# Two order lists for the start of a fused attention and MLP kernel: with two exponentials per unit, three MLP pieces in the list, and one doubling on GpSimd

## The chip, the cores and the metric

The kernel runs on one core of a Trainium2 chip. The time is device microseconds (us) of one execution. The core has engines that each work through their own instructions in order and meet through semaphores: TensorE (PE, with its weight loads shown as PEld), VectorE (DVE), ScalarE (ACT), GpSimd (POOL), and SyncE (SP), which here only issues transfers. POOL and ACT can issue transfers too.

## The reference

Eight batches, 12 heads, 448 positions, head size 64, model size 768, hidden size 3072. Cut to what matters:

```python
def rmsnorm(x, g):
    rms = np.sqrt(np.mean(x * x, axis=-1, keepdims=True) + 1e-06)
    return x / rms * g
q_n, k_n = rmsnorm(q, g_q), rmsnorm(k, g_k)
attn = softmax(q_n @ k_n.T / sqrt(64))        # per batch and head
x = concat_heads(attn @ v)                    # (8, 448, 768)
xn = (x - mean(x)) / np.sqrt(var(x) + 1e-06) * g_ln
out = x + np.maximum(xn @ w_ch1, 0.0) @ w_ch2 # 768 -> 3072 -> 768
```

## The kernel before

Heads are taken in pairs: 6 pairs per batch, 48 in all, numbered p = 0 to 47. Loading and preparation go by unit u: units 0 and 1 are one pair each, every other unit is two pairs (unit 4 is pairs 6 and 7, unit 5 is pairs 8 and 9). The 448 positions of a pair are cut into 7 groups: three of 128 per head and one with the last 64 of both heads.

Preparation of a unit has pieces with one-letter names (`pieces`, L188):

- `b` takes tiles, `a` squares k and `c` squares q (ACT), `d` and `e` sum these squares over the 64 elements of a row (DVE);
- `g` (`root`, L219) makes one over the root of both sums on ACT: a logarithm, then an exponential. Units 0 and 1 do this with 7 columns per kind, the others with 14. In the kernel before, one exponential makes both kinds, 128x28;
- `i` multiplies k with both gains (POOL from unit 2 on), `j` rounds it to 16 bits (POOL for units 1 to 5, then ACT), `k` makes the 16-bit rest (DVE);
- `l` scales q into `qn` (DVE), `m` doubles `qn` (POOL for units 1, 2 and 4, DVE for the others);
- `z` converts v (POOL). `L` loads a unit (SP); a load waits until the buffer of the unit two before it has been read.

For a pair, `K` and `Q` transpose keys and queries on PE into PSUM and copy them out (DVE; ACT for queries of pairs 0 and 1). `Sp.i` is a score matmul of group i and the exponential on ACT that reads its PSUM; the PSUM tiles of scores are two in turn, so score i+2 of the sequence waits for exponential i. The root of the keys is the exponential's scale, one number per row, so it is read long after unit preparation. `Vp.i` multiplies with the values; after `Vp.6`, DVE divides and writes the result into x (`evac_o`, L395: four instructions). `T` are statistics of x for the layer norm, `A` their sum, `N0` to `N2` the normalised rows of three tiles (DVE), `X0` to `X2` their transposes (PE) with copies (ACT, ACT, DVE), `R` the layer norm's root (ACT). `U0` to `U2` are the first three of 24 up pieces of the first MLP, one third of the columns at a time, in three PSUM tiles of a pool of three; the pieces after these use the same pool.

The order of the start, up to and including pair 6, is a list written out by hand, `ORDER` (L36). Every engine gets its instructions in the list's order. It holds batch 0's attention, the layer norm, pair 6, and the preparation of unit 5. After it, `run_rest` (L708) takes the MLP pieces of batch 0: 21 up pieces (6 matmuls 128x384 and a ReLU on ACT each) and 24 down pieces (6 matmuls each), and puts the attention steps of batch 1 between them:

```python
upto(int(min(goal, start + (goal - start) * done / (total - 960 * tail))))
```

`done` is the cost so far and `tail` is 13 pieces, so the 44 steps of batch 1 are spread evenly over the first 45 - 13 = 32 pieces. Step 1 is `b6 a6 i6` and the load of the first half of the down weights (`load_w2`, L529, issued by POOL behind `i6`); step 3 is `c6 S7.0`. The other half of the down weights comes with `a7 i7`. From pair 12 on DMA makes the transposes.

At the list's end, `M` makes two small numbers for a final test of ranges. With it come reductions `least` (L364): the least key root of a unit goes into `rr_all`, 25 columns, five of them at `M` for units 0 to 4, the others at the end of each unit's first pair. `flag` (L736) tests them in the last MLP.

Of the kernel before, what the change touches and what calls it, by code (L numbers as in the profile page):

```python
# [25 lines left out]
UNIT_PAIR = [PAIR_UNIT.index((u, 0)) for u in range(len(UNITS))]  # L26
EXP_BIAS = -4.0
WARM = 22
DVE_KG, POOL_HI, POOL_DUP, ACT_Q = (0, 1), (1, 2, 3, 4, 5), (1, 2, 4), (0, 1)

# [1 line left out]


ORDER = """  # L36
b0 a0 c0 L4 i0 j0 e0 k0 gq0 l0 b1 m0 a1 c1 K0 Q0 d0 G gk0 S0.0 S0.1 d1 e1 L5 i1 g1 j1 l1 k1 m1
z0 b2 a2 S0.2 d2 c2 S0.3 S0.4 K1 V0.0 e2 i2 S0.5 Q1 g2 l2 S0.6 S1.0 j2 V0.1 S1.1 S1.2 m2 b3
V0.2 a3 V0.3 k2 c3 S1.3 K2 V0.4 S1.4 z2 V0.5 Q2 S1.5 V0.6 V1.0 i3 W0 d3 e3 S1.6 V1.1 V1.2 S2.0
j3 T0 V1.3 S2.1 S2.2 Q3 V1.4 S2.3 K3 S2.4 V1.5 V1.6 S2.5 g3 z3 S2.6 V2.0 S3.0 S3.1 V2.1 k3  # L40
S3.2 b4 S3.3 V2.2 l3 a4 V2.3 m3 S3.4 V2.4 K4 S3.5 Q4 V2.5 V2.6 S3.6 Q5 S4.0 V3.0 S4.1 V3.1 i4
V3.2 d4 T1 K5 V3.3 W1 c4 V3.4 V3.5 S4.2 S4.3 V3.6 S4.4 S4.5 W2 e4 V4.0 V4.1 j4 S4.6 S5.0 k4
S5.1 g4 V4.2 l4 S5.2 V4.3 V4.4 V4.5 S5.3 K6 V4.6 z4 V5.0 S5.4 m4 b5 V5.1 G2 S5.5 L6 V5.2 S5.6
V5.3 V5.4 V5.5 Q6 a5 i5 V5.6 T3 T4 S6.0 S6.1 S6.2 S6.3 T5 S6.4 A V6.0 V6.1 N0 V6.2 N1 V6.3
S6.5 S6.6 d5 V6.4 X0 X1 U0 N2 R Q7 X2 c5 e5 j5 g5 k5 l5 z5 U1 U2 V6.5 M m5 V6.6 L7 K7
""".split()
DMA_UNIT = 8
PE_SET = (DMA_UNIT + 1) % 2
# [27 lines left out]
class _Fast:  # L76


    def __init__(self, ctx, tc, sh, q, k, v, gs, g_ln, w1, w2, out):
        self.gs, self.g_ln = gs, g_ln  # L80
        self.tc, self.nc, self.sh = tc, tc.nc, sh
        self.q, self.k, self.v, self.w1, self.w2, self.out = q, k, v, w1, w2, out
        nc = tc.nc
        pool = lambda name, bufs, **kw: ctx.enter_context(tc.tile_pool(name=name, bufs=bufs, **kw))
        self.p_in = pool("p_in", 2)
        self.p_n = pool("p_n", 2)
        self.p_e = pool("p_e", 2)
# [100 lines left out]
    def pieces(self, u):  # L188
# [29 lines left out]

        def root(n=slice(0, 2)):  # L219
            nc.scalar.activation(c["rt"][:, n], c["ssq"][:, n], AFT.Ln, bias=D * 1e-6)  # L220
            nc.scalar.activation(c["rb"][:, n], c["rt"][:, n], AFT.Exp, scale=-0.5)  # L221
# [85 lines left out]
    def trans_k(self, p):  # L307
        nc, sh = self.nc, self.sh
        u, w = PAIR_UNIT[p]
        qn, khl = self.units[u][0:2]  # L310
        kT, ps = self.kU[PE_SET][:, 960 * (p % 2):960 * (p % 2) + 960], self.tr
        nc.tensor.matmul(ps[:, 0:256].rearrange("p (e o) -> p e o", e=2)[:, :, 0:D],
                         khl[:, self.group(p, 6)], sh.id16, is_transpose=True, start=True, stop=False)
# [3 lines left out]
        nc.vector.tensor_copy(out=kT, in_=ps[:, 0:960])

    def trans_q(self, p):
        nc, sh = self.nc, self.sh  # L320
        u, w = PAIR_UNIT[p]
        qn, khl = self.units[u][0:2]
        tr = self.ps_m.tile([128, 1024], FP16, tag="mlp", name="psQ") if p < NPAIR else self.tr
        ps = tr[:, 128:128 + 2 * S].rearrange("p (e s) -> p e s", e=2)
        qT = self.qU[PE_SET][:, p % 2].rearrange("p e s -> p (e s)")
        nc.tensor.matmul(ps[:, :, 384:S], qn[:, self.group(p, 6)], sh.id16, is_transpose=True,
                         start=True, stop=False)
        for i in range(6):
            nc.tensor.matmul(ps[:, i // 3, ts(i % 3, 128)], qn[:, self.group(p, i)], sh.id16,  # L329
                             is_transpose=True, start=False, stop=(i == 5))  # L330
        if p in ACT_Q:
            nc.scalar.copy(out=qT, in_=ps.rearrange("p e s -> p (e s)"))
        else:
            nc.vector.tensor_copy(out=qT, in_=ps.rearrange("p e s -> p (e s)"))  # L334
        kT = self.kU[PE_SET][:, 960 * (p % 2):960 * (p % 2) + 960]
        self.prs[p] = dict(q=qT, main=kT[:, 192:960], left=kT[:, 0:192])

    def scores(self, p, i):
# [17 lines left out]
        g = self.group(p, i)  # L356
        nc.scalar.activation(out=c["E"][:, i], in_=ps[:, 0:S], func=AFT.Exp,  # L357
                             scale=self.units[PAIR_UNIT[p][0]][3][:, g:g + 1], bias=EXP_BIAS)
# [62 lines left out]
    def first_attention(self):  # L421
# [7 lines left out]
        for x in ORDER:  # L429
# [517 lines left out]
```

## Time and profile before

| what | value |
|---|---|
| median of 4 runs | 610.15 us (609.79 to 610.46) |
| the profiled execution | 609.62 us, span 607.9 us |
| PE busy | 579.5 us of the span |
| DVE, ACT, POOL busy | 287.1, 359.0, 189.6 us |
| first matmul | 9.81 us after the span's start |
| end of the list (last matmul of `K7`) | 59.60 us |

The page gives busy times and their share of the span by engine. Stretches ("windows") give the busy time of each engine between two times; the timeline gives instructions in order of time, and in brackets how long the engine was idle before one and what ended that. "L351" is a line of the kernel. In the timeline, instructions of the same form that follow each other are merged; a single one's duration can overlap the next by about 0.1 us, so distances between starts are used for sums.

### The profile page before, as it was taken

The numbers are of one execution on the slowest core, as the hardware profiler recorded it, in microseconds if no ns is written. First come the engines' busy times: TensorE is split into PE (matmuls) and PEld (weight loads), VectorE is DVE, ScalarE is ACT, GpSimd is POOL, SyncE is SP. The second block draws the span as 40 slices with busy tenths as digits, with TensorE's granted clock in tenths as the row PEclk, the third lists the DMA queues.
The fourth block names the chain that finished last, engine by engine and source line by source line (L and its number), as shares of the span: only waits on it lengthen the run. The fifth ranks groups of instructions, "written<-read, shape, count | busy, mean of one in ns | idle before, by whom it ended". The sixth has DMA issues, their size and how long they took to land.

```text
span 607.9 us, 11525 instructions
## 1 busy us (share of the span) xinstructions
PE 579.5 (95%) x4500; PEld 346.3 (57%) x4500; DVE 287.1 (47%) x643; ACT 359.0 (59%) x673; POOL 189.6 (31%) x245
## 2 busy tenths in 40 slices
PE   2777999999999999999999999999999999999995
PEld 1555566655566666655566666655566666654564
DVE  5798577734256255724266246633346322540011
ACT  5896887368843598448754498538754377114200
POOL 2844432232542355332552345514422000000000
PEclk9899999999999999999999999999999999999999
DMA  8999999679965486747865575948613330040011
GB/s 221 272 181 214 198 221 185 89 242 88 131 147 120 103 139 144 178 130 99 117 130 126 114 118 149 191 117 127 135 56 76 92 62 1 27 104 0 1 53 57
DMA packets 130861, 75.29 MB, mean 124 GB/s; under 512 B 96656, under 2 KB 121040, under 8 KB 130800
## 3 DMA queue, kind: packets, MB, share of 16 engines
q1 hardware_dynamic: 114048, 45.12, 38.9%
q0 software_dynamic: 16080, 28.94, 22.2%
q8 instruction: 37, 0.61, 0.4%
q10 hardware_dynamic: 672, 0.43, 0.2%
q14 instruction: 24, 0.20, 0.1%
HBM read 52.36 MB, written 11.01 MB: 104 GB/s over the span
## 4 chain that ended last, share of the span: by engine, by line
PE 89%; DVE 2%; ACT 0%; issue 0%; DVEq 0%
PE psC L647 36%; PE psH L631 35%; PE psS L351 8%; PE oA L389 5%; PE oB L391 2%; PE psS L354 1%; PE psS L355 1%; PE tr L329 0%; PE tr L315 0%; PE psU L677 0%; DVE stat L555 0%; DVE xn L576 0%; DVE x L406 0%; DVE qU L334 0%; ACT E L357 0%
## 5 line engine op out<-in xcount | busy, mean ns | idle before, releaser
L631 PE MATMUL psH<-xnT,w 128*128 128x512 f16 (+1 forms) x1134 | 241.9, 353 | 0.0
L357 ACT ACTIVATE E<-psS,rr_all 128x448 f16<-128x448 f32 x336 | 207.2, 634 | 49.6 <-PE psS L351 44.2
L647 PE MATMUL psC<-w,hT 128*128 128x384 f16 (+1 forms) x1368 | 234.7, 323 | 0.0
L633 ACT ACTIVATE hT<-psH 128x512 f16<-128x512 f32 (+1 forms) x189 | 103.9, 550 | 124.7 <-PE psH L631 123.1
L647 PEld LDWEIGHTS <-hT 128*128 128x128 f16 x1368 | 127.7, 98 | 74.4
L631 PEld LDWEIGHTS <-w 128*128 128x128 f16 x1134 | 102.7, 98 | 80.5
L351 PE MATMUL psS<-qU,kU 128*128 128x448 f16 x288 | 101.0, 358 | 8.0 <-ACT E L357 5.3
L389 PEld LDWEIGHTS <-E 128*128 128x128 f16 x1008 | 71.2, 99 | 48.8 <-issue 4.3
L228 POOL TENSOR_TENSOR qkv<-qkv,gprod 128x896 f32<-128x896 f32 x21 | 43.7, 2079 | 97.2 <-issue 50.6
L389 PE MATMUL oA<-v,E 128*128 128x65 f16 x864 | 67.0, 194 | 0.1
L651 DVE SCALAR_TENSOR_TENSOR x<-psC,rs_all,x 128x384 f32<-128x384 f32 x48 | 29.0, 616 | 71.0 <-PE psC L647 70.5
L404 DVE RECIPROCAL rec_all<-oA 128x6 f32<-128x6 f32 x48 | 9.3, 194 | 94.0 <-PE oA L389 93.8
L391 PE MATMUL oB<-v,E 128*128 128x65 f16 x288 | 52.0, 194 | 0.1
L127 POOL DMA_DIRECT2D qkv<-in_k_dram x14 | 11.2, 797 | 128.9 <-ACT E L357 77.0
L217 DVE TENSOR_REDUCE ssq<-khl 128x14 f32<-128x896 f32 (+1 forms) x24 | 25.6, 1065 | 45.6 <-ACT khl L214 45.5
L351 PEld LDWEIGHTS <-kU 128*128 128x128 f16 x288 | 28.2, 99 | 25.9 <-issue 6.1
L217 DVE TENSOR_REDUCE ssq<-qn 128x14 f32<-128x896 f32 (+1 forms) x25 | 26.1, 1046 | 21.9 <-ACT qn L214 21.8
L67 DVE SCALAR_TENSOR_TENSOR qn<-qkv,rr_all 128x256 f16<-128x256 f32 (+1 forms) x72 | 26.3, 425 | 15.3 <-ACT rr_all L221 15.3
L391 PEld LDWEIGHTS <-E 128*128 128x128 f16 x336 | 32.6, 97 | 0.3 <-DVE xl L411 0.2
L239 DVE TENSOR_TENSOR khl<-qkv,khl 128x896 f16<-128x896 f32 x21 | 22.7, 1083 | 10.6 <-ACT khl L236 6.9
L406 DVE TENSOR_TENSOR x<-oA,rec_all 128x384 f32<-128x384 f32 x48 | 26.8, 558 | 1.5
L555 DVE BATCH_NORM_STATS2 stat<-x 128x6 f32<-128x256 f32 (+1 forms) x75 | 26.2, 404 | 0.6
(104 smaller groups left out, 448.0 us busy)
## 6 DMA issues: line engine op xcount, KB each, us to landing
out_dram<-x SPq DMA_DIRECT2D x20, 384.0 KB, 2.5
qkv<-in_k_dram POOLq DMA_DIRECT2D x14, 384.0 KB, 3.8
qkv<-in_q_dram POOLq DMA_DIRECT2D x14, 384.0 KB, 5.1
qkv<-in_v_dram POOLq DMA_DIRECT2D x14, 384.0 KB, 7.1
w<-in_moe_w_ch_dram POOLq DMA_DIRECT2D x3, 1536.0 KB, 13.1
w<-in_moe_w_ch_dram POOLq DMA_DIRECT2D x2, 2304.0 KB, 25.5
qkv<-in_k_dram SPq DMA_DIRECT2D x7, 384.0 KB, 6.4
qkv<-in_q_dram SPq DMA_DIRECT2D x7, 384.0 KB, 5.9
```

What stands on the lines that cost most here:

```text
L67: nc.vector.scalar_tensor_tensor(out=out, in0=x, scalar=8.0, in1=r.unsqueeze(2).broadcast_to([x.shape[0], g, D]), op0=ALU.mult, op1=ALU.mult)
L217: nc.vector.tensor_reduce(out=c["ssq"][:, n], in_=c["sq", n], axis=AX.X, op=ALU.add)
L228: (nc.vector if u in DVE_KG else nc.gpsimd).tensor_tensor(out=c["t"][1], in0=c["t"][1], in1=sh.gprod.unsqueeze(1).broadcast_to([128, g, D] ...
L351: nc.tensor.matmul(ps[:, 0:S], c["main"][:, ts(i, 128)], q[:, ts(h, S)], start=True, stop=True)
L357: nc.scalar.activation(out=c["E"][:, i], in_=ps[:, 0:S], func=AFT.Exp, scale=self.units[PAIR_UNIT[p][0]][3][:, g:g + 1], bias=EXP_BIAS)
L389: nc.tensor.matmul(oA[:, t, cs], E[:, i, ts(t, 128)], rhs, start=(i == 0 and t == 0), stop=(i == 6 and t == 2))
L391: nc.tensor.matmul(oB[:, cs], E[:, i, 320:448], rhs, start=(i == 0), stop=(i == 6))
L406: nc.vector.tensor_tensor(out=x[:, :, 128 * hp:128 * hp + 128].rearrange("p t (e d) -> p t e d", e=2), in0=oA[:, :, :, 0:D], in1=rec[:, 0: ...
L631: nc.tensor.matmul(ps[:, 0:N], sh.w1[:, dc, ts(f, 128)], xnT[:, dc, 0:N], start=(dc == 0), stop=(dc == NDC - 1))
L633: nc.scalar.activation(out=hT[:, f, 0:N], in_=ps[:, 0:N], func=AFT.Relu)
L647: nc.tensor.matmul(ps[:, 0:g[1]], hT[:, f, ts(t, 128)], sh.w2[:, f, cols], start=(f == 0), stop=(f == NFF - 1))
L651: nc.vector.scalar_tensor_tensor(out=x[:, cols], in0=ps[:, 0:g[1]], scalar=self.rs[:, b, t:t + 1], in1=x[:, cols], op0=ALU.mult, op1=ALU.add)
```

## The change

- The list `ORDER` is another permutation of the same entries, with three new entries `C`. Each `C` emits the next MLP piece of batch 0 (up pieces 3, 4 and 5). One stands between `U2` and `V6.5`, one between `V6.6` and `R` (before `K7`), and one is the last entry.
- `run_rest` gets what is left: 18 up and 24 down pieces. The 44 steps of batch 1 are spread over 42 - 13 = 29 pieces.
- `m5` goes to POOL.
- `root` makes two exponentials, one for queries into a tile of two buffers, one for keys into `rr_all`, which now has a column for every row group of every pair (336). `least` is gone with its 25 reductions; `flag` tests 336 columns directly.

```diff
-DVE_KG, POOL_HI, POOL_DUP, ACT_Q = (0, 1), (1, 2, 3, 4, 5), (1, 2, 4), (0, 1)
+DVE_KG, POOL_HI, POOL_DUP, ACT_Q = (0, 1), (1, 2, 3, 4, 5), (1, 2, 4, 5), (0, 1)
 ORDER = """
-b0 a0 c0 L4 i0 j0 e0 k0 gq0 l0 b1 m0 a1 c1 K0 Q0 d0 G gk0 S0.0 S0.1 d1 e1 L5 i1 g1 j1 l1 k1 m1
-z0 b2 a2 S0.2 d2 c2 S0.3 S0.4 K1 V0.0 e2 i2 S0.5 Q1 g2 l2 S0.6 S1.0 j2 V0.1 S1.1 S1.2 m2 b3
-V0.2 a3 V0.3 k2 c3 S1.3 K2 V0.4 S1.4 z2 V0.5 Q2 S1.5 V0.6 V1.0 i3 W0 d3 e3 S1.6 V1.1 V1.2 S2.0
...
-S5.1 g4 V4.2 l4 S5.2 V4.3 V4.4 V4.5 S5.3 K6 V4.6 z4 V5.0 S5.4 m4 b5 V5.1 G2 S5.5 L6 V5.2 S5.6
-V5.3 V5.4 V5.5 Q6 a5 i5 V5.6 T3 T4 S6.0 S6.1 S6.2 S6.3 T5 S6.4 A V6.0 V6.1 N0 V6.2 N1 V6.3
-S6.5 S6.6 d5 V6.4 X0 X1 U0 N2 R Q7 X2 c5 e5 j5 g5 k5 l5 z5 U1 U2 V6.5 M m5 V6.6 L7 K7
+b0 L4 a0 i0 c0 j0 e0 k0 gq0 l0 m0 b1 c1 d0 G a1 K0 Q0 d1 gk0 e1 L5 i1 g1 S0.0 j1 l1 z0 k1 S0.1
+m1 b2 a2 S0.2 d2 V0.0 c2 S0.3 K1 e2 S0.4 i2 Q1 S0.5 g2 l2 S0.6 V0.1 j2 S1.0 V0.2 S1.1 S1.2 b3
+m2 V0.3 k2 z2 c3 V0.4 S1.3 K2 S1.4 a3 S1.5 i3 V0.5 Q2 V0.6 V1.0 V1.1 d3 e3 S1.6 V1.2 S2.0 W0
...
+S5.1 k4 g4 V4.2 S5.2 l4 V4.3 V4.4 V4.5 S5.3 K6 V4.6 z4 V5.0 S5.4 S5.5 m4 L6 b5 V5.1 G2 V5.2
+S5.6 Q6 V5.3 V5.4 V5.5 a5 V5.6 Q7 S6.0 T4 S6.1 T3 V6.0 S6.2 i5 S6.3 T5 S6.4 A V6.1 N0 N1 V6.2
+N2 V6.3 S6.5 S6.6 d5 V6.4 X0 X1 U0 X2 c5 e5 g5 j5 l5 z5 U1 U2 C k5 V6.5 V6.6 C M R K7 m5 L7 C
 """.split()
-        self.rr = fix.tile([128, len(UNITS)], FP32, name="rr_all", tag="rr_all")
+        self.rr = fix.tile([128, 7 * B * NPAIR], FP32, name="rr_all", tag="rr_all")
-            c["rb"] = self.p_n.tile([128, 2, 14], FP32, tag="rq", name="rr_all", bufs=6)[:, :, 0:g]
-            c["r", 0], c["r", 1] = c["rb"][:, 0], c["rb"][:, 1]
+            o = 7 * UNIT_PAIR[u]
+            c["r", 0] = self.p_n.tile([128, 14], FP32, tag="rq", name="rq")[:, 0:g]
+            c["r", 1] = self.rr[:, o:o + g]
         def root(n=slice(0, 2)):
             nc.scalar.activation(c["rt"][:, n], c["ssq"][:, n], AFT.Ln, bias=D * 1e-6)
-            nc.scalar.activation(c["rb"][:, n], c["rt"][:, n], AFT.Exp, scale=-0.5)
+            for i in range(2)[n] if isinstance(n, slice) else (n,):
+                nc.scalar.activation(c["r", i], c["rt"][:, i], AFT.Exp, scale=-0.5)
-        if i == 6 and UNIT_PAIR[u] == p and u > 4:
-            self.least(u)
-                for u in range(5):
-                    self.least(u)
+            elif key == "C":
+                self.chunks = self.chunks or self.mlp_chunks(0)
+                next(self.chunks)[1]()
-            chunks = list(self.mlp_chunks(b))
+            chunks = list(self.mlp_chunks(b) if b else self.chunks)
```

More of the change, by code (lines that the diff above doesn't have):

```diff
@@ L28 @@
 WARM = 22
-DVE_KG, POOL_HI, POOL_DUP, ACT_Q = (0, 1), (1, 2, 3, 4, 5), (1, 2, 4), (0, 1)
+DVE_KG, POOL_HI, POOL_DUP, ACT_Q = (0, 1), (1, 2, 3, 4, 5), (1, 2, 4, 5), (0, 1)
 ORDER = """
-b0 a0 c0 L4 i0 j0 e0 k0 gq0 l0 b1 m0 a1 c1 K0 Q0 d0 G gk0 S0.0 S0.1 d1 e1 L5 i1 g1 j1 l1 k1 m1
-z0 b2 a2 S0.2 d2 c2 S0.3 S0.4 K1 V0.0 e2 i2 S0.5 Q1 g2 l2 S0.6 S1.0 j2 V0.1 S1.1 S1.2 m2 b3
-V0.2 a3 V0.3 k2 c3 S1.3 K2 V0.4 S1.4 z2 V0.5 Q2 S1.5 V0.6 V1.0 i3 W0 d3 e3 S1.6 V1.1 V1.2 S2.0
-j3 T0 V1.3 S2.1 S2.2 Q3 V1.4 S2.3 K3 S2.4 V1.5 V1.6 S2.5 g3 z3 S2.6 V2.0 S3.0 S3.1 V2.1 k3
-S3.2 b4 S3.3 V2.2 l3 a4 V2.3 m3 S3.4 V2.4 K4 S3.5 Q4 V2.5 V2.6 S3.6 Q5 S4.0 V3.0 S4.1 V3.1 i4
-V3.2 d4 T1 K5 V3.3 W1 c4 V3.4 V3.5 S4.2 S4.3 V3.6 S4.4 S4.5 W2 e4 V4.0 V4.1 j4 S4.6 S5.0 k4
-S5.1 g4 V4.2 l4 S5.2 V4.3 V4.4 V4.5 S5.3 K6 V4.6 z4 V5.0 S5.4 m4 b5 V5.1 G2 S5.5 L6 V5.2 S5.6
-V5.3 V5.4 V5.5 Q6 a5 i5 V5.6 T3 T4 S6.0 S6.1 S6.2 S6.3 T5 S6.4 A V6.0 V6.1 N0 V6.2 N1 V6.3
-S6.5 S6.6 d5 V6.4 X0 X1 U0 N2 R Q7 X2 c5 e5 j5 g5 k5 l5 z5 U1 U2 V6.5 M m5 V6.6 L7 K7
+b0 L4 a0 i0 c0 j0 e0 k0 gq0 l0 m0 b1 c1 d0 G a1 K0 Q0 d1 gk0 e1 L5 i1 g1 S0.0 j1 l1 z0 k1 S0.1
+m1 b2 a2 S0.2 d2 V0.0 c2 S0.3 K1 e2 S0.4 i2 Q1 S0.5 g2 l2 S0.6 V0.1 j2 S1.0 V0.2 S1.1 S1.2 b3
+m2 V0.3 k2 z2 c3 V0.4 S1.3 K2 S1.4 a3 S1.5 i3 V0.5 Q2 V0.6 V1.0 V1.1 d3 e3 S1.6 V1.2 S2.0 W0
+V1.3 S2.1 Q3 V1.4 S2.2 K3 S2.3 j3 V1.5 S2.4 g3 T0 V1.6 S2.5 V2.0 S2.6 S3.0 S3.1 z3 V2.1 k3
+S3.2 b4 S3.3 a4 i4 l3 V2.2 V2.3 m3 S3.4 V2.4 K4 S3.5 Q4 V2.5 V2.6 S3.6 V3.0 c4 V3.1 Q5 S4.0
+S4.1 V3.2 d4 V3.3 T1 W1 K5 W2 V3.4 j4 S4.2 S4.3 V3.5 V3.6 S4.4 S4.5 S4.6 e4 V4.0 V4.1 S5.0
+S5.1 k4 g4 V4.2 S5.2 l4 V4.3 V4.4 V4.5 S5.3 K6 V4.6 z4 V5.0 S5.4 S5.5 m4 L6 b5 V5.1 G2 V5.2
+S5.6 Q6 V5.3 V5.4 V5.5 a5 V5.6 Q7 S6.0 T4 S6.1 T3 V6.0 S6.2 i5 S6.3 T5 S6.4 A V6.1 N0 N1 V6.2
+N2 V6.3 S6.5 S6.6 d5 V6.4 X0 X1 U0 X2 c5 e5 g5 j5 l5 z5 U1 U2 C k5 V6.5 V6.6 C M R K7 m5 L7 C
 """.split()
@@ L115, in __init__ @@
         self.units, self.loads, self.prs = {}, {}, {}
-        self.late, self.preps = [], {}
+        self.late, self.preps, self.chunks = [], {}, None
     def zero_left(self, u):
@@ L201, in begin @@
             c["rt"] = self.p_n.tile([128, 2, 14], FP32, tag="rt", name="rt")[:, :, 0:g]
-            c["rb"] = self.p_n.tile([128, 2, 14], FP32, tag="rq", name="rr_all", bufs=6)[:, :, 0:g]
-            c["r", 0], c["r", 1] = c["rb"][:, 0], c["rb"][:, 1]
+            o = 7 * UNIT_PAIR[u]
+            c["r", 0] = self.p_n.tile([128, 14], FP32, tag="rq", name="rq")[:, 0:g]
+            c["r", 1] = self.rr[:, o:o + g]
             c["qn"] = self.p_n.tile([128, 14, 2, D], FP16, tag="qn", name="qn")[:, 0:g]
             c["khl"] = self.p_n.tile([128, 14, 2, D], FP16, tag="khl", name="khl")[:, 0:g]
-            self.units[u] = (c["qn"], c["khl"], m, c["r", 1])
+            self.units[u] = (c["qn"], c["khl"], m)
         def square(n):
@@ L309, in trans_k @@
         u, w = PAIR_UNIT[p]
-        qn, khl = self.units[u][0:2]
+        qn, khl, m = self.units[u]
         kT, ps = self.kU[PE_SET][:, 960 * (p % 2):960 * (p % 2) + 960], self.tr
@@ L321, in trans_q @@
         u, w = PAIR_UNIT[p]
-        qn, khl = self.units[u][0:2]
+        qn, khl, m = self.units[u]
         tr = self.ps_m.tile([128, 1024], FP16, tag="mlp", name="psQ") if p < NPAIR else self.tr
@@ L355, in scores @@
             nc.tensor.matmul(ps[:, 0:S], left[:, 64:192], q[:, S:2 * S], start=False, stop=True)
-        g = self.group(p, i)
+        g = 7 * UNIT_PAIR[PAIR_UNIT[p][0]] + self.group(p, i)
         nc.scalar.activation(out=c["E"][:, i], in_=ps[:, 0:S], func=AFT.Exp,
-                             scale=self.units[PAIR_UNIT[p][0]][3][:, g:g + 1], bias=EXP_BIAS)
-        u = PAIR_UNIT[p][0]
-        if i == 6 and UNIT_PAIR[u] == p and u > 4:
-            self.least(u)
-    def least(self, u):
-        self.nc.vector.tensor_reduce(out=self.rr[:, u:u + 1], in_=self.units[u][3], axis=AX.X,
-                                     op=ALU.min)
+                             scale=self.rr[:, g:g + 1], bias=EXP_BIAS)
     def values(self, p, i):
```

## The prediction

> **What bounds the kernel now.** First the stretches of the whole span, then of the first 72 us:
>
> ```profile
> 8.00:16.00 8.00, 3.75 (x18) 1.89 (x19) 6.48 (x13) 6.22 (x16) 1.10 (x2) 1.00 1.08 316
> ...
> 40.00:48.00 8.00, 6.11 (x80) 3.85 (x77) 7.38 (x17) 6.53 (x14) 4.37 (x6) 1.00 1.11 203
> 48.00:56.00 8.00, 5.13 (x63) 3.39 (x63) 7.43 (x20) 6.71 (x13) 3.42 (x3) 1.00 1.11 223
> 56.00:64.00 8.00, 6.78 (x79) 5.11 (x79) 7.26 (x20) 4.73 (x11) 3.17 (x4) 1.00 0.70 188
> 64.00:72.00 8.00, 8.00 (x65) 5.09 (x64) 5.19 (x8) 7.62 (x17) 4.77 (x5) 1.00 1.05 200
> ```
>
> The columns are PE, PEld, DVE, ACT, POOL. From 64 us on PE is busy all the time; later stretches of 8 and 25 us show PE short by 0.13 and 0.11 us only. So an engine's saving after 64 us is worth nothing, and the time is PE's work plus PE's idle time before 64: 9.81 us before the first matmul and some 12 us behind it. In 24 to 64 us DVE is busy over 90%, ACT up to 48 nearly so. These two, with their waits for each other, make the 12 us.
>
> Second, the timelines of PE, DVE and ACT, for the places that the change touches:
>
> ```profile
> 16.14 0.53 PE L351 MATMUL psS<-qU,kU 128*128 128x448 f16 x1 [1.18 <-ACT E L357]
> 19.77 0.35 PE L351 MATMUL psS<-qU,kU 128*128 128x448 f16 x1 [0.24 <-ACT qU L332]
> 22.86 0.23 PE L312 MATMUL tr<-id,khl 128*128 128x128 f16 x1 [0.76 <-DVE khl L239]
> 23.73 0.56 PE L351 MATMUL psS<-qU,kU 128*128 128x448 f16 x1
> 26.87 0.35 PE L351 MATMUL psS<-qU,kU 128*128 128x448 f16 x1
> ...
> 63.39 0.55 PE L351 MATMUL psS<-qU,kU 128*128 128x448 f16 x2 [0.86 <-DVE kU L317]
> ```
> ```profile
> 25.29 0.62 DVE L334 COPY qU<-psQ 128x896 f16<-128x896 f16 x1 [0.90 <-PE psQ L329]
> 25.99 0.20 DVE L404 RECIPROCAL rec_all<-oA 128x6 f32<-128x6 f32 x1
> ...
> 46.78 0.62 DVE L334 COPY qU<-tr 128x896 f16<-128x896 f16 x1 [0.30 <-PE tr L329]
> ...
> 55.68 0.62 DVE L334 COPY qU<-tr 128x896 f16<-128x896 f16 x1 [0.52 <-PE tr L329]
> ...
> 62.67 0.66 DVE L317 COPY kU<-tr 128x960 f16<-128x960 f16 x1
> ```
> ```profile
> 19.88 0.23 ACT L221 ACTIVATE rr_all<-rt 128x28 f32<-128x28 f32 x1
> 20.01 2.21 ACT L357 ACTIVATE E<-psS,rr_all 128x448 f16<-128x448 f32 x4
> ```
>
> DVE runs without a gap from 25.29 to the 0.30 at 46.78: what starts it earlier moves all of this. The last PE gap, 0.86 us at 63.39, is `S7.0` waiting for the copy of `K7`, which DVE takes up only at 62.67. The score lines show PE slow (0.53) at 16, fast (0.35) at 19.77, slow again at 23.73 and fast at 26.87.
>
> Third, the transfers of the down weights:
>
> ```profile
> L530 POOL DMA_DIRECT2D w<-in_moe_w_ch_dram x2: 1465/1484/1502, 64.1 to 79.4; - x2
> DMA to landing us min/median/max: 24.1/25.5/26.9
> ```
>
> The first half is issued at 64.1 and lands at 88.2; PE takes up the first down piece at 92.34.
>
> **The change, part by part.** I follow the new list with distances between starts from before's timeline: score exponential 0.53, ReLU 0.38, square 0.84, logarithm 0.25, root's exponential 0.13 (19.88 to 20.01), DVE sum, scaling or rest 1.0, copies 0.55, division and writes 1.3, up piece on PE 0.98.
>
> *Two exponentials per unit.* One more on ACT for units 1 on: 0.13 each, four before 47 us, 0.5 together. After 64 us PE covers them. The four are counted in the walks here. The 25 reductions gone (0.36 for the five at 60.36) and `m5` off DVE (0.3) count in `K7`'s place. The wider test lies in the last MLP, where DVE is idle most of the time: nothing; without that cover it would be under 1 us.
>
> *9 to 26 us.* `g1` moves ahead of pair 0's first exponentials, from 14.27 to 12.85, so `l1` from 14.76 to 13.5, `k1` and with it `K1` from 16.47 to about 15.65. `z0` now stands before `m1` on POOL (0.82 + 0.64), so `m1` ends at 16.9, later than 16.3; but PE reaches `Q1` only there, 0.9 earlier than before's 17.83. `V0.0` now stands before `S0.3` on PE and waits for `z0`'s 15.0; `S0.3` is not due on ACT before 16.7. ACT gets to `g2` at 19.1, not 19.62, `l2` starts 0.6 earlier, and so does `K2` (22.2). Behind `K2` stand `S1.4` and `S1.5` and on ACT `a3`, which fills the 0.71 and 0.53 us that ACT idled there. `Q2`'s copy comes at 24.6, `V0.6`'s division at 25.2 in place of 25.99. So 0.8 earlier. Ends: 0.5 later (four exponentials on a full ACT and no move helps) to 1.2 earlier. I take 0.8, the walk's own.
>
> *26 to 47 us.* DVE's order is unchanged there and stays gapless, so the 0.8 carries through. `Q6` now comes before `V5.3` to `V5.5`, so the 0.30 idle at 46.78 goes. Pair 5's division starts at 46.2, before 47.32: 1.1 with both.
>
> *47 us to the end of the list.* `Q7`'s copy (0.55) moves ahead of the statistics; `N2` moves ahead of `d5` (1.0), and `X2` no longer waits for `Q7`'s copy (55.68). Walk on DVE: 46.25 + 1.3 + 0.55 + 2.15 (statistics) + 0.41 + 1.95 (`N0`, `N1`) = 52.6; `N2` 53.55; `d5` 54.55; `X2`'s copy, held by `U0`'s last third, 55.3; `e5` 56.3. On ACT `g5` then holds the three ReLUs of `U2` until 56.85, and the first `C` needs a PSUM tile from them: PE idles 0.5 before it. Then 0.98 + 0.35 + 0.98 + 0.39 + 0.98: the last `C` ends near 61.05. Before, PE had done the same work (three up pieces behind `K7`) at 62.53. So 1.5 in all, 0.4 from this part. Ends: 0 to 1.0.
>
> *`K7`.* DVE reaches its copy at 61.1 and `S7.0` is now behind two more up pieces, at 63.0: the 0.86 goes. `m5` on POOL (0.93 to 1.66 in the rows of L278) is done before `i6` can start, and SP's queue keeps its order.
>
> *Batch 1 in 29 pieces.* Here I book a cost. ACT was busy 7.62 of 8 us in 64 to 72. Before, the squares of unit 6 ran while PE stood still for `S7.0`; now PE goes on. ACT: ReLU, `a6` to 63.3, ReLU, `c6` to 64.5, then `S7.0`, ReLU, `S7.1`, ReLU, `j6`, and `S7.2` ends only at 67.7, while PE is at `S7.4`, which needs that PSUM tile, at 67.2. Waits: 0.12 at `S7.3`, 0.6 at `S7.4`, 0.2 at `S7.6`, about 0.95; at unit 7 the same pattern gives 0.2 more than now. Sum 1.15. Ends: 0 (before, `S7.5` got through with 0.05 us to spare) and 4.75 (0.95 at each of pairs 7 to 11).
>
> *Down weights.* Their issue follows `a6` and `i6`: 63.45 + 2.05 = 65.5, 1.4 later than now. With 24.1 us they land at 89.6; PE gets to the first down piece at 92.34 - 0.7 (one step moved behind it) - 1.2 = 90.45. 0.85 to spare: nothing. Ends: 0, and 1.95 with the 26.9 us of the second transfer. That one, issued near 79.6, lands at 106.5, before its use near 110.
>
> Sum: -0.8 - 0.3 - 0.4 - 0.85 + 1.15 = -1.2 us. The profiled execution took 609.62 (span 607.9 and 1.7 around it), 0.53 under the median; against the median, 610.15 - 1.2 gives **608.9 us**.
>
> The place where PE is slow is one more unknown, worth up to 1.2: were it fast from 22 to 26, DVE's run would start that much earlier. The Trainium skill, "TensorE: Matmul & The Clock Gate", Part 1, says that a window of about 3.4 us that runs freely decides on half or full clock, so the slow stretch would not be tied to the order. By rows the stretch stays where it is, 608.9; by that rule it may vanish, giving 607.7. The two rates, 0.53 to 0.56 and 0.35, agree with it; no run here shows its window.
>
> **The rivals.**
> - *No change within 0.2% (1.2 us, about what this kernel's measurement can tell from none).* The moves before 47 us bring nothing, since ACT and DVE have the same work there and were full already: -0.4 - 0.85 + 1.15 = -0.1, 610.0 us. Or the moves hold and the down weights take 26.9 us: -1.2 + 1.95, 610.9. For it: DVE over 90% busy. Against: 1.24 us of ACT idle at 25 to 27 that a moved square can fill.
> - *Slower.* ACT never catches up in batch 1: 44 steps over 29 pieces in place of 32, so each pair loses 0.95 us of PE as pair 7 does, 4.75 in place of 1.15: -2.35 + 4.75, **612.5 us**. It decides from 3.6 us of such waits on. For it: ACT at 7.0 to 7.6 of 8 us from 64 to 96. Against: only two of the five pairs share ACT with a unit's squares and ReLUs.
> - *Fast PE at 22 to 26*: 607.7, above.
>
> **How the numbers follow.** Forecast 0.36 and fast PE 0.09: faster 0.45. No change 0.33: the forecast lies near that border. Slower 0.22. Range 607.2 to 612.0: below, the fast PE with half of the crowding; above, most of the slower case. The forecast's own range is 607.9 to 609.6.
>
> **What would show it.** Right: `V0.6`'s division near 25.2; the first matmul of `S7.0` near 63.0 without a wait; short waits of PE for ACT at 65 to 71; no wait before the first down piece; batch 1 over at some 1.2 us before now. Wrong: `Q1` waiting for POOL beyond 17.8, PE gaps of over 2 us in 64 to 92, or a gap before the first down piece.

## The result: a little slower, and the profile after

The changed kernel took 610.71 us (median; 609.6 to 612.54) against 609.5 (607.95 to 610.82) for the kernel before: a ratio of **1.0022, interval 1.0017 to 1.0027**, or 1.3 us slower. The forecast was 608.9, 1.2 us faster. The profiled executions are 610.91 us (span 609.1) and 609.62 us (span 607.9), 1.29 apart, so the two traces hold the difference.

The stretches of after, PE, PEld, DVE, ACT, POOL:

```profile
48.00:56.00 8.00, 5.33 (x64) 3.33 (x63) 7.74 (x20) 6.45 (x11) 2.03 (x2) 1.00 1.11 222
56.00:64.00 8.00, 7.32 (x82) 5.45 (x80) 5.81 (x11) 3.90 (x13) 3.87 (x5) 1.00 0.77 206
64.00:72.00 8.00, 7.41 (x53) 4.40 (x51) 5.88 (x6) 7.97 (x18) 6.52 (x5) 1.00 0.77 160
72.00:80.00 8.00, 8.00 (x81) 5.38 (x80) 2.28 (x5) 6.86 (x14) 0.51 (x1) 1.00 1.27 214
80.00:88.00 8.00, 7.38 (x72) 4.76 (x70) 7.48 (x15) 7.24 (x17) 5.21 (x5) 1.00 1.24 236
```

PE stands still less than before up to 64 us (7.32 of 8 in place of 6.78), but is short by 0.59 in 64 to 72 and by 0.62 in 80 to 88, where it had been busy all the time. ACT is full in the first of the two, 7.97 of 8. The timeline of PE names the waits (last bracket; an idle time is marked from some 0.15 us on):

```profile
16.08 0.32 PE L381 MATMUL oA<-v,E 128*128 128x65 f16 x3 [1.44 <-POOL v L285]
...
24.36 0.53 PE L352 MATMUL psS<-qU,kU 128*128 128x448 f16 x1 [0.16 <-ACT E L358]
...
26.45 0.35 PE L352 MATMUL psS<-qU,kU 128*128 128x448 f16 x1
...
58.88 1.14 PE L624 MATMUL psH<-xnT,w 128*128 128x384 f16 x6 [0.68 <-ACT hT L674]
...
64.49 0.35 PE L352 MATMUL psS<-qU,kU 128*128 128x448 f16 x1
...
67.75 0.35 PE L352 MATMUL psS<-qU,kU 128*128 128x448 f16 x1 [0.17 <-ACT E L358]
...
69.49 0.35 PE L352 MATMUL psS<-qU,kU 128*128 128x448 f16 x1 [0.42 <-ACT E L358]
...
81.67 0.35 PE L352 MATMUL psS<-qU,kU 128*128 128x448 f16 x1 [0.46 <-ACT E L358]
```

`S7.0` at 64.49 waits for nothing: the 0.86 us for `K7`'s copy is gone. In its place PE waits for score exponentials at 67.75 (`S7.3`), 69.49 (`S7.4`) and 81.67 (`S9.1`). The ACT timeline of after shows why:

```profile
65.32 0.95 ACT L215 ACTIVATE qn<-qkv 128x896 f32<-128x896 f32 x1
66.16 0.63 ACT L358 ACTIVATE E<-psS,rr_all 128x448 f16<-128x448 f32 x1
66.67 0.50 ACT L626 ACTIVATE hT<-psH 128x384 f16<-128x384 f32 x1
67.05 0.65 ACT L358 ACTIVATE E<-psS,rr_all 128x448 f16<-128x448 f32 x1
67.56 0.52 ACT L626 ACTIVATE hT<-psH 128x384 f16<-128x384 f32 x1
67.93 0.98 ACT L237 ACTIVATE khl<-qkv 128x896 f16<-128x896 f32 x1
68.77 0.67 ACT L358 ACTIVATE E<-psS,rr_all 128x448 f16<-128x448 f32 x1
```

ACT works without a gap through `c6`, two exponentials, two ReLUs and `j6`. The exponential of `S7.2`, whose PSUM tile `S7.4` needs, starts only at 68.77, behind `j6`; PE has stood since 68.92 (the piece at 67.94 plus 0.98). The wait at `S7.3` stands behind the square `c6` in the same way, and at 81.67 it is a square again: `S9.1` needs the tile of `S8.6`, whose exponential stands behind `c7`:

```profile
80.13 0.97 ACT L215 ACTIVATE qn<-qkv 128x896 f32<-128x896 f32 x1
80.97 0.65 ACT L358 ACTIVATE E<-psS,rr_all 128x448 f16<-128x448 f32 x1
```

A balance by equal work, from distances between starts (an idle figure counts from the modelled end of a matmul, some 0.15 us later, so a wait is that much longer by starts). `K7`'s matmuls and three up pieces are through at 62.36 before (59.44 and three pieces of 0.97) and at 62.54 after (64.49 less two pieces): +0.2. The wait for `K7`'s copy, 0.86 marked, 1.03 by starts, is gone: -1.0. From `S7.0` to the first down piece: 28.95 us before (63.39 to 92.34, with 18 up pieces and one step more) and 28.29 after (64.49 to 92.78, 16 up pieces). Less two pieces of 0.98 and a step of 0.7, before comes to 26.29, so after lost 28.29 - 26.29 = **2.0 us** there. By starts they lie in six places: 0.33, 0.58 and 0.15 at `S7.3`, `S7.4` and `S7.6`, together 1.06 where before has 0.08, and 0.62, 0.24 and 0.25 at `S9.1`, `S9.4` and `Q10`, together 1.11 where before has 0.19. Sum: 0.2 - 1.0 + 2.0 = +1.2. The first up piece of batch 1 comes at 123.33 before and 124.42 after, 1.09 later; another 0.2 comes behind it up to the end of the profiled executions.

### The profile page after: what moved, and what is told of

The parts are those of the page before. It is cut to its first block, busy times and chain, and to the rows that moved or that the text cites. A ratio compares the mean times of both kernels' runs of the same rounds, so it can differ in the third digit from the quotient of the medians.

```text
span 609.1 us, 11525 instructions
## 1 busy us (share of the span) xinstructions
PE 580.5 (95%) x4500; PEld 346.7 (57%) x4500; DVE 286.5 (47%) x617; ACT 361.2 (59%) x697; POOL 190.5 (31%) x246
## 4 chain that ended last, share of the span: by engine, by line
PE 84%; DMA 2%; DVE 0%; SPq 0%; ACT 0%; issue 0%
PE psC L640 36%; PE psH L624 32%; PE psS L352 7%; PE oA L381 5%; DMA qkv<-in_q_dram 2%; PE oB L383 2%; PE psS L356 1%; PE psS L355 1%; PE tr L330 0%; SPq L135 0%; PE tr L316 0%; SPq L127 0%; ACT khl L215 0%; DVE kU L318 0%; DVE x L398 0%
## 5 line engine op out<-in xcount | busy, mean ns | idle before, releaser
L67 DVE SCALAR_TENSOR_TENSOR qn<-qkv,rq 128x256 f16<-128x256 f32 (+1 forms) x72 | 26.4, 426 | 15.6 <-ACT rq L223 15.6
```

What stands on the lines that cost most here:

```text
L67: nc.vector.scalar_tensor_tensor(out=out, in0=x, scalar=8.0, in1=r.unsqueeze(2).broadcast_to([x.shape[0], g, D]), op0=ALU.mult, op1=ALU.mult)
```

## The experiments

Theory 1: ACT is overtaken by the attention steps in batch 1. Theory 2, the rival: the new list is slower up to 47 us. Times are ratios to the kernel before. "To 110" is the distance from pair 5's division to the first matmul of the long run of down pieces behind batch 1's last step: 63.28 us before, 64.45 after. It leaves out the start, which the last section shows to vary by itself. The two ends in the kernel before (DVE's and PE's timelines):

```profile
47.32 0.19 DVE L404 RECIPROCAL rec_all<-oA 128x6 f32<-128x6 f32 x1
...
110.60 12.89 PE L647 MATMUL psC<-w,hT 128*128 128x384 f16 x78
```

### The three pieces alone, and the list without them

The first: the kernel before with three `C` at its list's end (and the code for `C`), so 29 pieces. The second: the changed kernel without its three `C`, so 32 pieces.

```diff
-... U1 U2 V6.5 M m5 V6.6 L7 K7
+... U1 U2 V6.5 M m5 V6.6 L7 K7 C C C
```


> The kernel before, its list unchanged, with three entries C appended behind K7: PE's order at the list's end is the same (three up pieces behind K7), but the 44 steps of batch 1 are now spread over 29 pieces in place of 32. Theory 1 (ACT is overtaken in batch 1): the wait of S7.0 for K7's copy goes (0.86 us), but PE waits for ACT's exponentials at 64 to 88 us for about 2.0 us, as in the changed kernel; total about +1.1 us over before (ratio 1.002). Theory 2 (the slower start of the new list is the cause, and the pieces are harmless): only the gain of 0.86 us is left, ratio 0.9985.


```diff
-... U1 U2 C k5 V6.5 V6.6 C M R K7 m5 L7 C
+... U1 U2 k5 V6.5 V6.6 M R K7 m5 L7
```


> The changed kernel without its three entries C; run_rest again emits 21 up pieces and spreads the steps over 32. Theory 1: the crowding of 2.0 us goes and the wait for K7's copy comes back in part (0.3 to 0.9 us): PE gets to the first down piece 1.0 to 1.5 us earlier than in the changed kernel, ratio to before 0.999 to 1.001. Theory 2: the start is as slow as in the changed kernel, ratio stays at 1.002.

The pieces alone: **1.0017** (1.0008 to 1.0026). The list and the exponentials without them: **0.9997** (0.9988 to 1.0006). PE's timeline of the first, then the only wait that is marked from 56 to 125 us in the second:

```profile
67.18 0.35 PE L351 MATMUL psS<-qU,kU 128*128 128x448 f16 x1 [0.17 <-ACT E L357]
...
68.92 0.35 PE L351 MATMUL psS<-qU,kU 128*128 128x448 f16 x1 [0.42 <-ACT E L357]
...
81.01 0.35 PE L351 MATMUL psS<-qU,kU 128*128 128x448 f16 x1 [0.46 <-ACT E L357]
```
```profile
61.70 0.55 PE L352 MATMUL psS<-qU,kU 128*128 128x448 f16 x2 [0.88 <-DVE kU L318]
```

The same three waits, to the hundredth, stand in the old list as soon as the pieces move, and none in the new list without them. The loss comes with the three pieces. The list without them is even 0.42 us shorter to 110 than before (62.86).

### The old start, and the two exponentials alone

The changed kernel with the old list's first 101 entries (up to `S3.3`); then the kernel before with two exponentials, the wide `rr_all` and no `least`.

```diff
-b0 L4 a0 i0 c0 j0 e0 k0 gq0 l0 m0 b1 c1 d0 G a1 K0 ... S3.2 b4 S3.3
+b0 a0 c0 L4 i0 j0 e0 k0 gq0 l0 b1 m0 a1 c1 K0 ... S3.2 b4 S3.3
```


> The first 101 entries (up to S3.3, some 33 us) in before's order, the rest as in the changed kernel. Theory 1: the start decides little: V0.6's division came 0.22 us later in the changed kernel (26.21 against 25.99), so 0.2 us are won back, ratio 1.002. Theory 2: 1.0 to 1.5 us are won back, ratio 1.000.


```diff
-            nc.scalar.activation(c["rb"][:, n], c["rt"][:, n], AFT.Exp, scale=-0.5)
+            for i in range(2)[n] if isinstance(n, slice) else (n,):
+                nc.scalar.activation(c["r", i], c["rt"][:, i], AFT.Exp, scale=-0.5)
```


> The kernel before with its own list, without pieces C and with unit 5's doubling on DVE, but with two exponentials per unit, fixed places for the key roots and no reductions at M. Theory 1 (PE waits for ACT in batch 1 because three pieces were taken out of it): the exponentials cost 0.13 us each on ACT and stand in gaps; ratio 0.999 to 1.001. Rival (the added ACT work itself makes ACT the bound, in the start and at units 6 and 7): 0.5 to 1.0 us slower, ratio 1.0008 to 1.0016.

The old start: 1.0017 (1.0008 to 1.0026), with the same waits of 0.17, 0.42 and 0.46. The exponentials: 1.0000 (0.9991 to 1.0009). Theory 2, which had 1.000 for the old start, falls, and the exponentials cost nothing that can be measured.

### Squares early, rounding on GpSimd, and another pace

Three ways to spare ACT, each on the changed kernel: unit 6's squares in the list, units 6 and 7's rounding (`j`) on POOL, and fewer steps per up piece; then all together.

```diff
-U1 U2 C k5 V6.5 V6.6 C M R K7 m5 L7 C
+U1 U2 C b6 c6 k5 V6.5 V6.6 C M R K7 a6 m5 L7 C
```


> The changed kernel with c6 put behind the first C and a6 behind K7, so that ACT does the two squares of unit 6 (0.84 us each) in the 0.46 to 0.83 us gaps that it has between the ReLUs at 60 to 63 us. Theory 1: ACT is 1.7 us less behind at 64 us, PE's waits at 67 to 71 us (1.2 us by distances between starts) go, those at 81 to 86 us stay: 1.0 to 1.2 us faster than the changed kernel, ratio to before 1.000. Theory 2: no difference from the changed kernel, 1.002.


```diff
-POOL_HI = (1, 2, 3, 4, 5)
+POOL_HI = (1, 2, 3, 4, 5, 6, 7)
```


> The changed kernel with the 16-bit rounding of the keys of units 6 and 7 on POOL in place of ACT: 0.84 us of ACT less in each of the two places where PE waits for exponentials; nothing else moves but POOL's order. Theory 1: PE's waits at 69 us (0.42) and 81 to 86 us (0.46 and two short ones) go: 0.8 to 1.5 us faster than the changed kernel, ratio 1.000 to 1.001. Rival (ACT's own load does not set it): 1.002 as the changed kernel.


```diff
-                done += cost
+                done += cost * ((0.85 if i < 18 else 1.25) if b == 0 else 1.0)
```


> The changed kernel; the 44 steps still end with the 29th piece, but an up piece, which has a ReLU on ACT, counts 0.85 and a down piece 1.25: 1.29 steps per up piece in place of 1.52. Theory 1: the waits of PE for exponentials at 67 to 86 us shrink from some 1.8 us to 0.5 us or less, ratio to before 0.9995 to 1.0005. Rival (ACT is behind because of the two squares alone, whatever the pace): under 0.4 us better than the changed kernel, ratio 1.0015 to 1.002.

The three edits in one kernel:

> The changed kernel with the two squares of unit 6 moved into the list, the rounding of units 6 and 7 on POOL and the pace by ACT together. Theory 1: no wait of PE for an exponential is left behind the list's end; what remains over before is the gain of 0.86 us at K7's copy: ratio 0.998 to 0.9995, faster than before. Rival (part of the loss lies elsewhere, in the list or the pieces): 1.000 or more.

Squares early: 1.0012 (1.0003 to 1.0021). Rounding on POOL: 1.0010 (1.0001 to 1.0019). Pace: **1.0030** (1.0018 to 1.0042), worse. All three: 1.0019 (1.0010 to 1.0028). PE's timelines, squares early, then rounding on POOL, then the pace:

```profile
69.41 0.35 PE L352 MATMUL psS<-qU,kU 128*128 128x448 f16 x1 [0.20 <-ACT E L358]
...
81.58 0.35 PE L352 MATMUL psS<-qU,kU 128*128 128x448 f16 x1 [0.46 <-ACT E L358]
```
```profile
85.45 0.22 PE L327 MATMUL tr<-id,qn 128*128 128x128 f16 x1 [0.85 <-DVE kU L318]
```
```profile
67.42 0.35 PE L352 MATMUL psS<-qU,kU 128*128 128x448 f16 x1 [0.59 <-ACT E L358]
...
83.40 0.35 PE L352 MATMUL psS<-qU,kU 128*128 128x448 f16 x1 [0.63 <-ACT E L358]
```

Taking work off ACT wins 0.6 to 0.7 us by the ratios, where 1.0 to 1.2 and 0.8 to 1.5 were expected; the intervals still overlap the change's own, so this is likely and not more. The squares early leave one wait of 0.20 at unit 6, and unit 7's stays. With the rounding on POOL the two waits behind the squares `c6` and `c7` stay (0.17 and 0.46), the one behind `j6` is gone, and one of 0.85 for a copy on DVE is new. The pace was a clear miss. ACT had fewer steps per up piece and PE waited longer, 0.59 and 0.63, and as the steps had to be packed into the down pieces, about half of its loss (by starts 1.5 of 3.2 us of waits) lies at 99 to 108 us. All three together, with the pace in them, missed their 0.998 to 0.9995 too (a wait of 0.63 at 82.04). So theory 1 in its first form, that the mean rate of steps in the up pieces is too high for ACT, falls. The lower pace had put two steps side by side at `[e6 S7.1][j6 S7.2 K8]` and `[e7 S9.0][j7 S9.1 ...]`, right beside ACT's squares and roundings. That gave theory 1a: not the rate decides, but where two steps stand together. Theory 1b is the rest of theory 1: the mean rate does, and waits that are removed here come back later.

### The place of the doubled steps

With 44 steps over 29 pieces (or 32), some pieces have two steps behind them. Where ACT prepares units 6 and 7, after's doubles fall on `[d6][c6 S7.0]`, `[j6 S7.2 K8][g6 v6 S7.3]` and `[e7 S9.0][j7 S9.1 ...]`; before's on `[c6 S7.0][e6 S7.1]`, `[k6 S7.4 Q8][l6 S7.5]` and `[j7 S9.1 ...][g7 v7 S9.2 ...]`. First, the changed kernel at its own rate with a table that, but for its first place, has single steps where units 6 and 7 use ACT; second, the same with the squares early; third, the kernel before at its own rate, 32 pieces, with after's two places doubled.

```diff
-                upto(int(min(goal, start + (goal - start) * done / (total - 960 * tail))))
+                upto(AT[min(i, 28)] if b == 0 else
+                     int(min(goal, start + (goal - start) * done / (total - 960 * tail))))
+AT = (2, 3, 4, 5, 6, 7, 9, 11, 13, 14, 15, 16, 17, 18, 19, 21, 23, 25, 27, 29, 31, 32, 34, 36, 37, 39, 41, 42, 44)
```


> The changed kernel with the 44 steps still spread over 29 pieces, but by a table: wherever ACT has a square, a rounding or a root of units 6 and 7 (steps 2 to 7 and 15 to 19) one step per piece, and the places with two steps (15 of 29 pieces) behind these. Theory 1a (PE waits where two steps stand together beside ACT's preparation work; the mean rate is harmless): the waits at 67 to 70 and 81 to 86 us fall from 1.8 us to 0.6 or less, ratio to before 0.9995 to 1.001. Theory 1b (the mean rate over the whole of batch 1 is too much for ACT or DVE, so that the waits come back elsewhere): new waits at 95 to 110 us, ratio 1.0015 or more.

With the squares early as well:

> The same table and the two squares of unit 6 in the list (c6 behind the first C, a6 behind K7). Theory 1a: nearly no wait of PE for ACT is left between 64 and 92 us, and the gain of 0.86 us at K7's copy shows: ratio 0.9985 to 1.000. Theory 1b: 1.001 or more.


```diff
+AT = (1, 2, 4, 6, 7, 8, 9, 11, 12, 13, 15, 16, 18, 19, 20, 22, 23, 24, 26, 27, 28, 30, 31, 33, 34, 35, 37, 38, 39, 41, 42, 44)
```


> The kernel before, 44 steps over 32 pieces as before, but two places with two steps are moved by a piece or two, onto the roundings of units 6 and 7 on ACT: steps 5 and 6 behind the fourth piece (before 7 and 8 behind the sixth) and steps 17 and 18 behind the thirteenth (before 18 and 19 behind the fourteenth). Theory 1a (the place of the doubled steps makes the waits, at whatever mean rate): PE waits 0.4 to 1.0 us in all at 64 to 69 and 79 to 82 us, ratio 1.0005 to 1.0015. Theory 1b (the mean rate makes them): 0.9995 to 1.0003.

After's rate, doubles moved: 1.0008 (0.9999 to 1.0017). With the squares too: 1.0008 (0.9999 to 1.0017), no better, where 0.9985 to 1.0 was expected. The kernel before with nothing but the doubles shifted: **1.0018** (1.0009 to 1.0027). PE's timelines of the first and the third:

```profile
70.45 0.35 PE L356 MATMUL psS<-qU,kU 128*128 128x448 f16 x1 [0.29 <-ACT E L359]
...
84.92 0.35 PE L353 MATMUL psS<-qU,kU 128*128 128x448 f16 x1 [0.27 <-ACT E L359]
```
```profile
62.75 0.55 PE L352 MATMUL psS<-qU,kU 128*128 128x448 f16 x2 [0.86 <-DVE kU L318]
...
66.21 0.35 PE L352 MATMUL psS<-qU,kU 128*128 128x448 f16 x1 [0.20 <-ACT E L358]
...
79.22 0.35 PE L352 MATMUL psS<-qU,kU 128*128 128x448 f16 x1 [0.46 <-ACT E L358]
```

At before's rate, same list, same pieces, a loss nearly as large as the change's comes with the place of two doubles alone (to 110: 63.99, 0.71 more than before), beside a `K7` wait that is still there. At after's rate 0.0014 of the 0.0022 goes when they are moved (by the one profile less, 64.07 to 110 against 64.45). So the place of the doubles is shown to make a loss of this size. What keeps the moved table 0.0008 above before, although its `K7` wait is gone, can be read from its trace, if not separated by a run. By starts its waits where units 6 and 7 use ACT fell from 2.2 us to 0.9, and the wait of 0.68 before the first `C` is still there. But at 95 to 105 us it waits some 0.95 us, in gaps of 0.3 and less, where before waits 0.12 and after nothing; of its last 14 pieces eleven have two steps behind them, in after eight. That is the sign that theory 1b had named, new waits at 95 to 110: moving the doubles removes part of the waits and brings part of them back, so the rate is not cleared.

### Whether `K7`'s wait is worth having

The changed kernel removes the 0.86, and so does the list of before with `K7` taken forward. Four lists ask what that is worth alone, and with unit 6's squares out of ACT's way. The last entries are:

```diff
-... X2 c5 e5 j5 g5 k5 l5 z5 U1 U2 V6.5 M m5 V6.6 L7 K7
+... X2 c5 e5 j5 g5 z5 U1 U2 K7 k5 l5 V6.5 M m5 V6.6 L7
+... X2 c5 b6 c6 e5 j5 g5 z5 U1 U2 K7 a6 k5 l5 V6.5 M m5 V6.6 L7
+... X2 c5 e5 j5 g5 z5 U1 U2 K7 b6 a6 k5 l5 V6.5 M m5 V6.6 L7
+... X2 c5 e5 j5 g5 z5 U1 U2 K7 b6 a6 k5 l5 V6.5 M m5 V6.6 c6 L7
```


> The kernel before, with K7 put behind U2 and ahead of k5 and l5, so that its copy no longer stands behind DVE's preparation of unit 5; no pieces, steps over 32. It measures the disputed gain by itself: S7.0 no longer waits. If the 0.86 us at 63.39 are a free gain: ratio 0.9985 to 0.999. If ACT needs that time for the squares of unit 6, as Theory 1 has it, PE waits for exponentials at 66 to 70 us instead: 0.9995 to 1.0005.

> The kernel before with K7 ahead of k5 and l5, and the two squares of unit 6 in the list: c6 behind c5, where ACT otherwise waits 2.65 us for DVE, a6 behind K7. No pieces, steps over 32. Theory 1: the wait at K7's copy is a free gain only if ACT's squares are done by then; here they are, so neither the 0.86 us for DVE nor the 0.59 us for ACT that took its place with K7 alone are left: ratio 0.9980 to 0.9990, the fastest so far. Rival (something else holds PE there): 0.9995 to 1.0005.

> The list of before, 32 pieces, K7 behind U2 and the square of unit 6's k (b6, a6) behind K7, ahead of V6.5. When only K7 was moved, the wait of 0.86 us for K7's copy was replaced by one of 0.59 us for ACT at the third score matmul, behind the two squares. If ACT's load just there is what eats the gain, then taking one square (0.84 us) ahead of the scores takes away the 0.59 and nothing comes in its place: ratio 0.9985 to 0.9992 (0.5 to 0.9 us). If DVE and ACT are both full up to here, so that what one is spared the other waits for, the wait only goes elsewhere (the ReLUs behind the square, the copies behind the sum): ratio 0.9995 to 1.0010.

> As the kernel with K7 and a6 moved, and the square of unit 6's q (c6) behind V6.6 as well, some 3 us later than in the list that waited 3.46 us for q's transfer; it should be landed by then. If ACT's load at the first scores of batch 1 decides: ratio 0.9982 to 0.9992, no wait of PE for ACT from 62 to 70 us. If the wait only goes elsewhere: 0.9995 to 1.0010. If q is still not there when ACT comes to it, PE waits for ACT near 61 us, and it is slower than the kernel with a6 alone.

In this order: 0.9996 (0.9986 to 1.0006); **1.0101** (1.0086 to 1.0116); 1.0014 (1.0003 to 1.0024), outside both of its expected ranges; 1.0001 (0.9992 to 1.0010). The second is confounded: `c6` came before its data. Its ACT and PE timelines:

```profile
57.89 0.95 ACT L214 ACTIVATE qn<-qkv 128x896 f32<-128x896 f32 x1 [3.46 <-DMA qkv<-in_q_dram]
```
```profile
60.48 1.87 PE L677 MATMUL psU<-xnT,w 128*128 128x128 f16 x18 [4.01 <-DVE xnT L618]
```

It says nothing of `K7`. The first and the last do; PE's timeline of `K7` alone, then of `K7` with both squares, later:

```profile
63.74 0.35 PE L351 MATMUL psS<-qU,kU 128*128 128x448 f16 x1 [0.59 <-ACT E L357]
...
118.90 4.06 PE L647 MATMUL psC<-w,hT 128*128 128x384 f16 x24 [0.21 <-DVE x L651]
```
```profile
66.15 0.22 PE L326 MATMUL tr<-id,qn 128*128 128x128 f16 x1 [0.44 <-DVE kU L317]
...
118.42 4.06 PE L647 MATMUL psC<-w,hT 128*128 128x384 f16 x24 [0.47 <-DVE x L651]
```

With `K7` alone, 0.59 of the 0.86 comes back as a wait for ACT, and to 110 the list has won 0.12 (63.16). With both squares out of the way it has won 0.52 by then (62.76), and loses 0.47 at 118.42. That second wait is new: it is for the write of x that frees a PSUM tile of the down pieces. The ACT and DVE timelines of the last list:

```profile
108.91 0.95 ACT L214 ACTIVATE khl<-qkv 128x896 f32<-128x896 f32 x1 [1.47 <-DMA kU<-khl]
```
```profile
109.89 1.08 DVE L217 TENSOR_REDUCE ssq<-khl 128x14 f32<-128x896 f32 x1 [1.95 <-ACT khl L214]
...
113.97 2.81 DVE L576 SCALAR_TENSOR_TENSOR xn<-x,stat,gln 128x768 f16<-128x768 f32 x3
116.69 1.02 DVE L576 SCALAR_TENSOR_TENSOR xn<-xl,stat,gln 128x768 f16<-128x768 f32 x1
117.74 1.14 DVE L651 SCALAR_TENSOR_TENSOR x<-psC,rs_all,x 128x384 f32<-128x384 f32 x2
```

The square of unit 9's k waits for a transfer out of the tile that it overwrites (DMA transposes of K), its sum stands in front of the division and of batch 1's whole layer norm on DVE, and only behind that comes the write at 117.74. From pair 5's division to that write it is 71.50 us; before, 71.44 (47.32 to 118.76):

```profile
118.76 1.14 DVE L651 SCALAR_TENSOR_TENSOR x<-psC,rs_all,x 128x384 f32<-128x384 f32 x2
```

The chain did not come forward at all, while PE did. Before had no slack there: its own down piece was released by this write and started at 119.43, 0.06 us later than the spacing of the run gives. In the last list the whole gain is gone at the first up piece of batch 1, 76.07 us after pair 5's division against 76.01. With `a6` alone ACT's 0.59 stayed (at 63.73), and at 119.38 PE waited 0.69: unit 9's square came 63.3 us after pair 5's division, in the last list 62.7, before 62.6. The chain is not fixed: in the changed list without the pieces the transfer landed earlier, the square came after 62.1 us, PE did not wait at 118, and at the first up piece of batch 1 that list was still 0.48 us ahead (75.53), though its 0.9997 does not tell this from nothing. What sets the landing is not tested. So the gain of `K7`'s wait is real up to 110 us, part of it if ACT is not relieved, and in these lists the chain at 118, a transfer and DVE's work behind it, takes the rest back. None of the lists is measurably faster than the kernel before.

## Why the prediction was wrong

By its own steps:

- *Two exponentials*, nothing but the 0.5 us in the walks: right; alone they gave 1.0000.
- *9 to 26 us*, -0.8: wrong, and the largest miss. The division meant to come at 25.2 came at 26.21, before at 25.99. `V0.0`, which the new list puts ahead of `S0.3` and `K1` on PE, waited 1.44 us (marked at 16.08) for `z0`, which the walk had finished at 15.0; it began only at 15.20, as its data came late. That the data would be there was taken without a row. POOL's timeline, then that of the changed list without the pieces, where they were there:

```profile
15.20 0.83 POOL L285 CAST v<-w 128x768 f16<-128x768 f32 x1 [0.68 <-DMA w<-in_v_dram]
```
```profile
14.03 0.83 POOL L285 CAST v<-w 128x768 f16<-128x768 f32 x1
```

  In that run, with PE slow near 23 us as in before and after, the division came 15.52 us after the first matmul; in after 16.79, in the three runs of the old list with such a PE 16.1 to 16.3. So some 0.6 to 0.8 us of the walk seem to be there when v lands in time; but that is one of the eight runs of the new list, and a comparison of executions, not a test. Over the profiled executions, the mixed start left out, the division comes at 25.48 on average with the new list (eight kernels) and at 25.24 with the old one (eight): 0.2 lost in place of 0.8 won.
- *26 to 47 us*, -0.3: right. From `V0.6`'s division to pair 5's it is 21.09 us after and 21.33 before, 0.24 less, and the same to 0.02 in every run of the two lists. With the step before it, pair 5's division came at 47.30, before at 47.32, and on average at 46.56 and 46.57: no gain is left of the 1.1.
- *47 us to the end of the list*, -0.4: mis-sized. By starts, from pair 5's division to the end of three up pieces it is 15.04 us before, 15.24 after, and 14.50 in the list without the pieces. So the moves on DVE gain 0.5, and the first `C`, which stands right behind `U2`, gives it back with a wait of 0.84 by starts (0.68 marked), which was walked as 0.5.
- *`K7`*, -0.86: right; the wait went. What the four lists add is that the rule taken at the outset, that the time is PE's work plus its idle time before 64, does not hold by itself: ACT from 63 to 70 and the chain at 118, without slack before, stop a PE that is earlier. In after the crowding comes ahead of that chain, and PE gets there late enough not to wait.
- *Batch 1 in 29 pieces*, +1.15: the right mechanism and place, mis-sized. At pair 7 it was right, 1.06 by starts for 0.95, with the three waits that were walked (0.33, 0.58 and 0.15 for 0.12, 0.6 and 0.2). At pair 9, put at 0.2 more than now without a walk, it was 0.9 more (1.11 for 0.19). Together 2.0 by equal work. It was set down as a matter of the rate; the runs show the place of the doubled steps, and do not clear the rate.
- *Down weights*, 0: right. Issued at 67.16, later than the 65.5 told, they landed 20.0 to 24.1 us later, and no wait stands before the first down piece at 92.78.

So the sum becomes +0.2 - 0.2 + 0.2 - 1.0 + 2.0 = +1.2 in place of -0.8 - 0.3 - 0.4 - 0.85 + 1.15 = -1.2, against 1.29 between the profiled executions. The steps that failed are the start (by 1.0), the end of the list (by 0.6) and the crowding (by 0.85, most of it at pair 9). The outcome is the "slower" rival in direction, but not in its size (612.5): only pairs 7 and 9, which share ACT with a unit's squares and rounding, pay, as the argument against it said; behind 92.8 us after waits 0.1. The rival "fast PE at 22 to 26" is treated below. That the time lies inside the stated range is luck: its upper part stood for a "slower" case in which all five pairs pay.

## What to carry to other kernels

Where steps are spread evenly over pieces, a changed count moves the places at which two of them fall together, and with two PSUM tiles in turn it is these places beside the long instructions of the engine that empties them that cost time, at an unchanged mean rate too; look up which steps fall there before booking the gain of a moved piece. A wait that goes is a gain only up to the next engine that has no slack: follow it through the stages behind, here to a transfer and DVE's chain 50 us later. A step that is put forward in a list is only worth what its data allow: look up when they land, in more than one execution. And a move at the start is not worth walking to a tenth when the first transfers land a microsecond apart from one execution to the next.

## What the runs showed of the hardware

- The same list runs through the start at two speeds. Seven kernels have the same entries up to 47 us. From the first matmul to pair 5's division three of them took 37.4 to 37.6 us and four 36.6 to 36.7. In the three, score matmuls near 23 us took 0.56; in the four, 0.35. One line of each kind, from the PE timelines of the lists with `K7` and both squares, and with `K7` and `a6`:

```profile
22.81 0.56 PE L351 MATMUL psS<-qU,kU 128*128 128x448 f16 x1
```
```profile
23.60 0.35 PE L351 MATMUL psS<-qU,kU 128*128 128x448 f16 x1
```

  The granted clock of the stretch 24 to 28 us is 0.70 in the kernel before, one of the three, and 1.00 in the list with `K7` and `a6`. So the fast PE of the prediction's rival exists and is worth 0.9 us with the old list, but it comes by the execution, with the old list and with the new one. The Trainium skill, "TensorE: Matmul & The Clock Gate", Part 1, says that the window that decides on the clock runs freely and that the number of slow matmuls differs from run to run; the traces agree, by the 0.9 us. No run here shows the window itself.
- A slow stretch can come later. In the kernel with the squares early the granted clock of 52 to 56 us is 0.65, and 18 matmuls of `U0` take 2.13 us, with PE busy 3.23 of 4 us around them; before had 1.00 there. This profile reads 65.04 to 110, more than after's 64.45, while its ratio of 1.0012 is below the change's 1.0022: a single profile can mislead by more than the change is worth.
- The first matmul comes between 8.80 and 10.01 us in these seven kernels, though nothing ahead of it differs.
